# Value product split by head into single PSUM banks from batch 2 on, with two planner costs changed (causal attention followed by an MLP, one core)

## The chip, the cores and the metric

The kernel runs on one core of a Trainium2 chip. The metric is the device time in microseconds (us). TensorE (PE) does the matmuls, VectorE (DVE) and ScalarE (ACT) work on what they leave in PSUM, GpSimd (POOL) converts types and issues some loads, SyncE (SP) issues most of the DMA. PSUM, where matmuls write, is used as 8 banks of 512 float32 values in each of 128 partitions.

## The reference

Block-causal attention over 8 batches of 8 heads, 576 positions and a head size of 64, then an MLP with the activation h * sigmoid(beta * h) over all 4608 rows:

```
scores = q @ k^T / sqrt(64)                       # [8, 8, 576, 576]
scores = where(pos_i // 64 >= pos_j // 64, scores, -1e9)
attn   = softmax(scores)
x      = (attn @ v) as rows of 512 (8 heads x 64)  # [4608, 512]
h      = x @ w_in                                 # 512 -> 2048
g      = h * sigmoid(beta * h)
out    = g @ w_out                                # 2048 -> 512, float32
```

## The kernel before

**Two streams of work.** Attention runs over 32 units, one for each batch b and head pair c (u = 4b + c). The MLP runs over 9 chunks of 512 rows (r = 0 to 8). Attention's result is written transposed into xT, from which the chunks read; a chunk can start once the batches that hold its rows are done. Both streams are mixed on PE.

**One attention unit.** K and Q are converted to bfloat16 and transposed into QKT (in batches 0 and 1 by PE and a copy on DVE, from batch 2 on by DMA). The score product (L708, helper L443) works with 64-row tiles, the two heads of a pair side by side on the two halves of the array. It is done in visits: groups 0 to 2 of a unit take a pair of banks each, group 3 a small block in a single bank. From batch 2 on (JOIN) two units share three visits: groups 0 and 1 of the first, groups 2 and 3 of both, groups 0 and 1 of the second. ACT takes the exponential of a bank pair (L724, 128 x 1024) into E, DVE sets masked blocks to zero (L730, L732). The value product (L764) then multiplies E with V, full 128-row tiles, 15 matmuls of 65 columns for each head: 64 values and a row sum from a column of ones. Before the change both heads are one operation of 30 matmuls on a pair of banks. DVE takes reciprocals of the row sums (L776, 128 x 10) and multiplies (L783, 128 x 640) into xq; for unit 1 alone, ACT does the multiplication as ten scaled copies (L788). From batch 3 on a DMA transposes xq into xT (L800); in batches 0 to 2 PE transposes it (L813) and DVE, or ACT for units 2 and 3, copies it (L823, L821).

**One MLP chunk.** 16 groups of four matmuls of 512 columns (L1000), one bank each; ACT takes a tanh (L1010), DVE forms the gate gT (L1014), and the bank is free. The output product of chunk 0 is plain (L1036). Chunks 1 to 8 use a seven-product scheme on quadrants (function fast: products at L921, 8 matmuls of 256 columns for each half of rows; sums of quadrants on DVE at L885; results out of PSUM on ACT at L942 and DVE at L945 and L936). One of its banks is held through four products in a row, a second one for the others.

**What sets the order.** Class Plan holds a list scheduler that runs when the kernel is built. Each operation has engines, a duration, a latency, a priority and tiles; the scheduler goes forward in time and gives each free engine the ready operation of the lowest priority number. The order of each engine and the buffers' places are fixed by it; on the chip each engine goes through its own list and waits on semaphores. On PE a change between row tiles and full tiles costs the constant SWITCH (L53) in the plan, an operation of the other mode has 0.25 added to its priority number, and an operation counts as ready only SLACK (L54) after its inputs. Filler matmuls (L523, L525) are put in while PE has nothing else in the first 50 us.

**Banks.** The class of a PSUM tile decides where it may lie. "PP" is a pair, at the first free place of its list `at` (by default 0 or 2). "P1" is a single bank, and while any pair is still to come it may be one of 4 to 7 only (L246):

```
ok = [k for k in banks if k >= 4 or pairs == 0]
t.slot = next((k for k in ok if k ^ 1 not in banks), ok[0])
```

Score groups are PP at 0 or 2. The value product is PP with a list of its own (L754), from batch 2 on 0, 2, 4, 6 in this order. L1000, the output products, PE's transposes and the small score block are P1.

Of the kernel before, what the change touches and what calls it, by code (L numbers as in the profile page):

```python
# [4 lines left out]
ACT = mybir.ActivationFunctionType  # L5
# [43 lines left out]
class Plan:  # L49


    SEM = 70.0
    SWITCH = 140.0  # L53
    SLACK = 120.0  # L54
    LAND = 2600.0
    PKT, BOTH, LATE = 97.0, 0.87, 2000.0
# [303 lines left out]
def bass_blockwise_causal_attn__then__act_swish_beta_kernel(  # L360
# [10 lines left out]
    with es:  # L371
# [6 lines left out]
        PARTS = [((0, 4, "SP", range(6)), (4, 8, "SP", range(2)), (4, 8, "POOL", range(2, 6)))] + [((0, 8, "SP", range(6)),)] * 7  # L378
        GROUPS = [((0,), (1,), (2,), (3,))] + [((0, 1), (2, 3))] * 7
        NS = 6  # L380
        JOIN = (2,3,4,5,6,7)
        NO = 4
        FAST = range(1, NRC)
# [68 lines left out]
        def xq_(tx):  # L452
            return 3 if tx.cls == "XX" else tx.slot
# [147 lines left out]
        for u in range(NU):  # L601
# [157 lines left out]
            def fav(g, e, te=te, pv=pv, Tv=Tv, c=c):  # L759
                for h in range(2):  # L760
                    for i in range(5):
                        for t in range(i + 1):
                            o = PS[:, pv.slot + h, 65 * i:65 * i + 65]
                            z = g.matmul(o, eblk(te, t, i, h), Vn[Tv.slot][:, t, 2 * c + h, 0:65],  # L764
                                         start=(t == 0), stop=(t == i))
                return z
# [4 lines left out]
            def both(pv, n0, n1):  # L771
                a = PS[:, pv.slot, n0:n1]
                return bass.AP(a.tensor, a.offset, [a.ap[0], [512, 2], [65, 5], [1, n1 - n0]])

            def fr(g, e, pv=pv, ti=ti):
                return g.reciprocal(inv[ti.slot][:].rearrange("p (h i n) -> p h i n", h=2, n=1), both(pv, 64, 65))  # L776

            r = P.op("DVE", 150, fr, deps=[av], tiles=[pv, ti], prio=0)

            def fm(g, e, pv=pv, ti=ti, tx=tx):  # L780
                x = inv[ti.slot][:]
                x = bass.AP(x.tensor, x.offset, [x.ap[0], [5, 2], [1, 5], [0, 64]])
                return g.tensor_tensor(xq[xq_(tx)][:].rearrange("p i (h d) -> p h i d", h=2), both(pv, 0, 64), x,  # L783
                                       ALU.mult)
            def fa(g, e, pv=pv, ti=ti, tx=tx):
                for h in range(2):
                    for i in range(5):
                        z = g.activation(xq[xq_(tx)][:, i, 64 * h:64 * h + 64], PS[:, pv.slot + h, 65 * i:65 * i + 64],  # L788
                                         ACT.Copy, scale=inv[ti.slot][:, 5 * h + i:5 * h + i + 1])
                return z  # L790
# [339 lines left out]
```

## Time and profile before

| | |
|---|---|
| median of 4 runs | 333.69 us (333.17 to 336.76) |
| the profiled execution, its own time | 333.85 us |
| its span, first to last instruction | 332.0 us |
| granted TensorE clock | 1.00 |
| PE, DVE, ACT, POOL busy | 323.9, 220.9, 212.9, 85.2 us |
| L1000 | 576 matmuls of 512 columns |
| L921 | 896 matmuls of 256 columns |
| L764 (value product) | 960 matmuls of 65 columns |
| first L1000 starts at | 28.82 us |
| DMA engines' mean busy share | 0.9 or more from about 8 to 232 us, 0.2 or less after |

Lines of the profile name an engine, the line of the kernel, the operation, what is written and read, the shape and the count. Matmuls overlap, so the duration of one (379 ns for 512 columns) is longer than the distance from one start to the next; for the pace of PE the starts are what counts. A wait is put down to what came last before it ended. "issue" is time in which an engine waited for nothing that the profile shows.

### The profile page before, as it was taken

The page shows a single profiled execution, that of the slowest core. Times are in us where ns is not written, and L with a number is a line of the kernel's source. Part 1 is how long each engine was busy: PE and PEld are TensorE (multiplying, and loading weights), DVE is VectorE, ACT ScalarE, POOL GpSimd, SP SyncE. Part 2 cuts the span into 40 slices and gives each one's busy share as a digit, 9 for nine tenths or more (in the row PEclk, how much of TensorE's full clock was granted, in tenths as well). Part 3 has the DMA queues.
Part 4 walks back from the last instruction along what each step waited for, and adds up shares of the span by engine and source line. Part 5 has one row for each costly group of instructions (what it writes and reads, how often), then busy time and mean ns, then how long its engine had stood idle before and what let it go on. Part 6 is the DMA issues. An engine that isn't in the chain of part 4 may idle for free.

```text
span 332.0 us, 7512 instructions
## 1 busy us (share of the span) xinstructions
PE 323.9 (98%) x3146; PEld 203.8 (61%) x3090; DVE 220.9 (67%) x448; ACT 212.9 (64%) x324; POOL 85.2 (26%) x127
## 2 busy tenths in 40 slices
PE   7998999999999999999999999999999999999996
PEld 4574455545586457754765666576566766666685
DVE  4647875678653887358956694668467685666742
ACT  2876974297558886768657866874875555544521
POOL 7656082055074036103520631060000000000000
PEclk9999999999999999999999999999999999999999
DMA  7999999999999999999999999999102210110023
GB/s 210 226 233 235 187 210 210 202 280 211 185 258 203 205 231 195 194 214 200 174 173 221 240 207 185 171 179 167 35 34 40 86 51 34 53 43 32 1 96 126
DMA packets 154993, 53.41 MB, mean 161 GB/s; under 512 B 139072, under 2 KB 154448, under 8 KB 154960
## 3 DMA queue, kind: packets, MB, share of 16 engines
q1 hardware_dynamic: 141200, 40.19, 65.2%
q10 hardware_dynamic: 8192, 8.39, 8.5%
q0 software_dynamic: 5568, 4.36, 8.3%
q8 instruction: 24, 0.39, 0.5%
q14 instruction: 9, 0.07, 0.1%
HBM read 36.71 MB, written 9.44 MB: 139 GB/s over the span
## 4 chain that ended last, share of the span: by engine, by line
PE 91%; DMA 3%; ACT 2%; issue 1%; DVE 1%; SPq 1%; POOL 0%
PE PS L1000 38%; PE PS L921 29%; PE PS L708 8%; PE PS L764 8%; PE PS L1036 4%; DMA ST<-in_k_dram 2%; PE PS L525 1%; PE PS L813 1%; ACT E L724 1%; DMA xT<-xq 1%; PE PS L634 1%; ACT xq L788 1%; SPq L618 1%; ACT th L1010 0%; POOL QKn L625 0%
## 5 line engine op out<-in xcount | busy, mean ns | idle before, releaser
L1000 PE MATMUL PS<-xT,w_in 128*128 128x512 bf16 x576 | 136.6, 379 | 0.6 <-DMA xT<-xq 0.4
L1010 ACT ACTIVATE th<-PS,beta 128x512 f32<-128x512 f32 x144 | 96.6, 699 | 60.6 <-PE PS L1000 59.4
L1014 DVE SCALAR_TENSOR_TENSOR gT<-th,PS 128x512 f16<-128x512 f32 x144 | 95.1, 681 | 32.0 <-ACT th L1010 31.1
L724 ACT ACTIVATE E<-PS 128x1024 bf16<-128x1024 f32 x93 | 92.1, 1028 | 27.7 <-PE PS L708 27.7
L1000 PEld LDWEIGHTS PS<-xT,w_in 128*128 128x128 bf16 x576 | 53.3, 98 | 56.3 <-DVE gT L1014 2.0
L921 PE MATMUL PS<-w_out,gT 128*128 128x256 f16 x512 | 63.0, 273 | 0.0
L921 PEld LDWEIGHTS PS<-w_out,gT 128*128 128x128 f16 x512 | 49.0, 98 | 12.1 <-issue 1.3
L574 POOL CAST Vn<-Vs 128x640 bf16<-128x640 f32 (+1 forms) x28 | 22.3, 797 | 96.0 <-DMA Vs<-in_v_dram 94.6
L665 POOL CAST QKn<-ST 128x640 bf16<-128x640 f32 x48 | 36.4, 759 | 28.1 <-DMA ST<-in_k_dram 14.7
L708 PE MATMUL PS<-QKT 64*128 64x320 bf16 (+4 forms) x328 | 36.4, 297 | 0.2 <-ACT E L724 0.2
L764 PEld LDWEIGHTS PS<-Vn,E 128*128 128x128 bf16 x930 | 30.8, 97 | 3.9 <-DVE E L730 0.4
L942 ACT ACTIVATE ost<-PS 128x512 f32<-128x512 f32 x32 | 19.4, 606 | 21.5 <-PE PS L921 21.5
L921 PE MATMUL PS<-OV 128*128 128x256 f16 x256 | 31.9, 273 | 0.0
L764 PE MATMUL PS<-Vn,E 128*128 128x65 bf16 x930 | 31.9, 193 | 0.0
L708 PEld LDWEIGHTS PS<-QKT 64*128 64x128 bf16 (+1 forms) x328 | 13.4, 95 | 25.7 <-issue 11.2
L921 PEld LDWEIGHTS PS<-OV 128*128 128x128 f16 x256 | 24.2, 98 | 5.8 <-issue 1.1
L783 DVE TENSOR_TENSOR xq<-PS,inv 128x640 bf16<-128x640 f32 x30 | 24.6, 821 | 0.8
L885 DVE TENSOR_TENSOR OV<-gT 128x1024 f16<-128x1024 f16 x32 | 23.6, 744 | 1.1 <-PE PS L921 0.6
L730 DVE MEMSET E<- 64x64 uint32 x62 | 6.9, 112 | 23.8 <-ACT E L724 21.7
L945 DVE SCALAR_TENSOR_TENSOR ost<-PS,ost 128x512 f32<-128x512 f32 x22 | 15.1, 688 | 8.7 <-PE PS L921 6.2
L921 PE MATMUL PS<-OV,gT 128*128 128x256 f16 x128 | 16.1, 273 | 0.0
L1036 PE MATMUL PS<-w_out,gT 128*128 128x512 f16 x64 | 15.5, 380 | 0.0
(65 smaller groups left out, 175.3 us busy)
## 6 DMA issues: line engine op xcount, KB each, us to landing
out_dram<-ost ACTq DMA_DIRECT2D x32, 256.0 KB, 4.3
ST<-in_q_dram SPq DMA_DIRECT2D x12, 576.0 KB, 5.8
ST<-in_k_dram SPq DMA_DIRECT2D x12, 576.0 KB, 7.7
Vs<-in_v_dram SPq DMA_DIRECT2D x24, 256.0 KB, 5.0
ST<-in_q_dram SPq DMA_DIRECT2D x8, 288.0 KB, 6.4
ST<-in_k_dram SPq DMA_DIRECT2D x8, 288.0 KB, 6.8
w_in<-in_moe_w_in_dram POOLq DMA_DIRECT2D x4, 512.0 KB, 10.9
w_out<-in_moe_w_out_dram POOLq DMA_DIRECT2D x4, 512.0 KB, 9.7
```

Of the source, the lines that this page charges most:

```text
L574: return g.tensor_copy(Vn[t.slot][:, 0:n, g0:g1, 0:64], Vs[ts.slot][:, 0:n, g0:g1, :])
L665: return g.tensor_copy(QKn[tn.slot][:].rearrange("p a w n -> p (a w n)")[:, 640 * (2 * a + w):][:, 0:640] .rearrange("p (t h d) -> p t h d ...
L708: z = g.matmul(o, QKT[tqk.slot][r, uu % 2, 1, 128 * t + y:128 * t + m + y], x)
L724: return g.activation(E3[es_(te)][:, g0, :, :], PS[:, ps.slot:ps.slot + 2, :], ACT.Exp, scale=0.125)
L764: z = g.matmul(o, eblk(te, t, i, h), Vn[Tv.slot][:, t, 2 * c + h, 0:65], start=(t == 0), stop=(t == i))
L783: return g.tensor_tensor(xq[xq_(tx)][:].rearrange("p i (h d) -> p h i d", h=2), both(pv, 0, 64), x, ALU.mult)
L885: return P.op("DVE", dve_t(SZ * HC / 2), mk(lambda g: g.tensor_tensor(fo(), fx(), fy(), op)), deps=deps, tiles=tiles, prio=prio)
L921: x = g.matmul(PS[:, pw.slot, HM * w:HM * w + HM], fa()[:, j, 128 * w:128 * w + 128], fb()[:, j, :], start=first and (pair or w == 0) and ...
L1000: z = g.matmul(PS[:, ph.slot, :], w_in[:, c, 128 * j:128 * j + 128], xT[:, c, row % RX:row % RX + RC], start=(c == 0), stop=(c == 3))
L1010: return g.activation(th[tt.slot][:], PS[:, ph.slot, :], ACT.Tanh, scale=beta[:, j:j + 1])
L1014: return g.scalar_tensor_tensor(out=gT[tg.slot][:, j, :], in0=th[tt.slot][:], scalar=1.0, in1=PS[:, ph.slot, :], op0=ALU.add, op1=ALU.mult)
L1036: z = g.matmul(PS[:, po.slot, 0:d1 - d0], gT[tg.slot][:, j, 128 * w:128 * w + 128], w_out[:, j, d0:d1], start=(j == 0), stop=(j == NJ - 1))
```

## The change

From batch 2 on (HALVES) each head of the value product is an operation of its own: 15 matmuls into one P1 bank, then its own reciprocal of 5 row sums for each partition and its own multiplication of 320 values into the head's columns of xq. What follows (transposing xq) waits for both. In batches 0 and 1 the value product stays whole, on a PP tile. In the plan, a value matmul is set at 30 ns in place of 34, and SWITCH at 97 ns in place of 140. The scaled copies on ACT for unit 1 are gone; DVE does that multiplication as for the others.

```diff
-    SWITCH = 140.0
+    SWITCH = 97.0
...
+        HALVES = (2,3,4,5,6,7)
...
-            pv = P.tile("PP")
-            pv.at = (4, 6, 0, 2) if u in (2, 3) else (4, 6) if b < 1 else (0, 2, 4, 6) if b in JOIN else (0, 2)
+            whole = b not in HALVES
             ti, tx = P.tile("inv"), P.tile("XX" if u == 3 else "xq")
...
-            av = P.op("PE", 30 * 34, fav, deps=ex + zs + load[u], tiles=[te, Tv, pv, ti, tx],
-                      lat=30 * 34 + 180, mode="full", prio=pr(u)+.4 + 5 * (b < 1))
...
-            if u in (1,):
-                m = P.op("ACT", 1500, fa, deps=[av, r], tiles=[pv, ti, tx], lat=1700, prio=0)
-            else:
-                m = P.op("DVE", dve_t(640), fm, deps=[av, r], tiles=[pv, ti, tx], prio=0)
+            nrm = []
+            for hs_ in ((0, 1),) if whole else ((0,), (1,)):
+                pv = P.tile("PP" if whole else "P1")
+                pv.at = (4, 6, 0, 2) if u in (2, 3) else (4, 6) if b < 1 else (0, 2, 4, 6) if b in JOIN else (0, 2)
+
+                def fav(g, e, te=te, pv=pv, Tv=Tv, c=c, hs_=hs_):
+                    for h in hs_:
+                        for i in range(5):
+                            for t in range(i + 1):
+                                o = PS[:, pv.slot + h - hs_[0], 65 * i:65 * i + 65]
+                                z = g.matmul(o, eblk(te, t, i, h), Vn[Tv.slot][:, t, 2 * c + h, 0:65],
+                                             start=(t == 0), stop=(t == i))
+                    return z
+
+                nh = len(hs_)
+                av = P.op("PE", 15 * nh * 30, fav, deps=ex + zs + load[u], tiles=[te, Tv, pv, ti, tx],
+                          lat=15 * nh * 30 + 180, mode="full", prio=pr(u)+.4 + 5 * (b < 1))
...
+                def fr(g, e, pv=pv, ti=ti, hs_=hs_, both=both):
+                    x = inv[ti.slot][:, 5 * hs_[0]:5 * hs_[-1] + 5]
+                    return g.reciprocal(x.rearrange("p (h i n) -> p h i n", i=5, n=1), both(pv, 64, 65))
+
+                r = P.op("DVE", 150, fr, deps=[av], tiles=[pv, ti], prio=0)
+
+                def fm(g, e, pv=pv, ti=ti, tx=tx, hs_=hs_, nh=nh, both=both):
+                    x = inv[ti.slot][:, 5 * hs_[0]:5 * hs_[0] + 5]
+                    x = bass.AP(x.tensor, x.offset, [x.ap[0], [5, nh], [1, 5], [0, 64]])
+                    y = xq[xq_(tx)][:].rearrange("p i (h d) -> p h i d", h=2)[:, hs_[0]:hs_[-1] + 1]
+                    return g.tensor_tensor(y, both(pv, 0, 64), x, ALU.mult)
+                m = P.op("DVE", dve_t(320 * nh), fm, deps=[av, r], tiles=[pv, ti, tx], prio=0)
                 m.same = [r]
-            nrm = [m]
+                nrm.append(m)
```

More of the change, by code (lines that the diff above doesn't have):

```diff
@@ L757, in bass_blockwise_causal_attn__then__act_swish_beta_kernel @@
                 spare_x = tx
[L759 to L766, printed above, removed]
-            av = P.op("PE", 30 * 34, fav, deps=ex + zs + load[u], tiles=[te, Tv, pv, ti, tx],
-                      lat=30 * 34 + 180, mode="full", prio=pr(u)+.4 + 5 * (b < 1))
@@ L771, in both @@
[L771 to L790, printed above, removed]
-            if u in (1,):
-                m = P.op("ACT", 1500, fa, deps=[av, r], tiles=[pv, ti, tx], lat=1700, prio=0)
-            else:
-                m = P.op("DVE", dve_t(640), fm, deps=[av, r], tiles=[pv, ti, tx], prio=0)
+            nrm = []
@@ new lines, in bass_blockwise_causal_attn__then__act_swish_beta_kernel, with both @@
+            for hs_ in ((0, 1),) if whole else ((0,), (1,)):
[12 more added lines that the diff above has]
+                          lat=15 * nh * 30 + 180, mode="full", prio=pr(u)+.4 + 5 * (b < 1))
+                def both(pv, n0, n1, nh=nh):
+                    a = PS[:, pv.slot, n0:n1]
+                    return bass.AP(a.tensor, a.offset, [a.ap[0], [512, nh], [65, 5], [1, n1 - n0]])
+                def fr(g, e, pv=pv, ti=ti, hs_=hs_, both=both):
[8 more added lines that the diff above has]
+                m = P.op("DVE", dve_t(320 * nh), fm, deps=[av, r], tiles=[pv, ti, tx], prio=0)
```

## The prediction

> **What bounds the kernel now.** I read the page's table of engines first, then its slices, then the chain that ended last, and after that the waits of TensorE alone.
>
> ```profile
> PE 323.9 (98%) x3146; PEld 203.8 (61%) x3090; DVE 220.9 (67%) x448; ACT 212.9 (64%) x324; POOL 85.2 (26%) x127
> ...
> PE   7998999999999999999999999999999999999996
> ...
> PE 91%; DMA 3%; ACT 2%; issue 1%; DVE 1%; SPq 1%; POOL 0%
> ```
>
> TensorE (PE) is busy in nearly every slice but the first four and the last, and it carries 91% of the chain. No other engine is above 67%. A busy PE need not be a full PE, so the second view is where PE waited at all:
>
> ```profile
> PE PS L523 <- POOL identF L459: 2.4, 1, 2.4
> PE PS L813 <- issue: 1.1, 1, 1.1
> ...
> PE PS L1000 <- DMA xT<-xq: 0.4, 1, 0.4
> ```
>
> Those few microseconds are nearly all there is. The third view is the order of time on PE, to see whether the matmuls follow each other at their own rate:
>
> ```profile
> 107.27 1.07 PE L764 MATMUL PS<-Vn,E 128*128 128x65 bf16 x30
> 108.17 2.75 PE L1000 MATMUL PS<-xT,w_in 128*128 128x512 bf16 x12
> 110.86 0.39 PE L708 MATMUL PS<-QKT 64*128 64x512 bf16 x2
> 111.08 0.19 PE L443 MATMUL PS<-QKT 64*128 64x64 bf16 x2
> 111.11 0.35 PE L708 MATMUL PS<-QKT 64*128 64x448 bf16 x2
> 111.40 0.82 PE L1000 MATMUL PS<-xT,w_in 128*128 128x512 bf16 x3
> ```
>
> Start to start, the value product's 30 matmuls take 108.17 - 107.27 = 0.90 us, 30 ns each. The chain has eight matmuls of L1000 in 1.73 us, 216 ns each; so the 12 here should take 2.59 us, and the score product (L708) starts 2.69 us after their start: 0.10 us for the change of tile mode. The way back costs the same: 111.40 - 111.11 is 0.29 us, of which two 448-column matmuls side by side account for about 0.19 us. Doing this sum for every neighbouring pair from 30 us on leaves only five gaps of 0.15 us or more: 0.55 us at 202.5 (input of chunk 5 not landed), 0.43 at 53.0, 0.25 at 99.7, 0.17 at 44.3 and 0.15 at 34.8, together 1.55 us. So after 30 us the time is the number of matmuls, plus mode changes, plus 1.55 us. Before 30 us PE waits for data, exponentials and normalised rows; the first L1000 starts at 28.82 us.
>
> **What the Trainium skill says.** TensorEngine Tiling (Array Packing), Key Properties: changing the tiling mode drains TensorE. The trace agrees, with 0.10 us each way. PSUM — Partial Sum Buffer, the section on bank collisions: two engines may not use one bank at once. So VectorE (DVE) can only read a finished head while PE works on the other because each has its own bank; no collision is in this trace. Perfetto Trace Analysis, Optimizing Scalar/DVE Operations: if the vector engine isn't saturated but causes bubbles on other engines, smaller instructions may complete work sooner. Here the first half holds (67%), but the trace has hardly any bubble on PE to remove.
>
> **The change part by part.** I sum against the profiled execution's own 333.85 us (span 332.0 and 1.85 around it); the median of the runs shown is 333.69, 0.16 less.
>
> *Numbers of the planner.* Mode change 140 to 97 ns and 34 to 30 ns for a value matmul cost no time on the chip; they are what the trace above shows. They move the order on PE. Every visit of the score product in batches 2 to 7 needs both bank pairs 0-1 and 2-3, and each can be filled again only after two exponentials of 1.03 us (L724), so visits cannot join: three for each two head pairs, 36 in all, 72 mode changes or about 7 us, before and after. The gain open here is the gaps from orders planned with wrong times: at most 1.55 us. I take 0.9 of it, the gap at 202.5 and a part of the rest, since that one is a landing that was due by a slow plan of PE. Ends: 0 and 1.55.
>
> *Two half products.* The same 30 matmuls, 0.45 us for each half. In this trace the matmuls of one operation follow those of another at the normal rate, so 24 more borders cost PE nothing in themselves. What is new is the place: a half asks for one of banks 4 to 7, which L1000, the output products and the small score block share, where the pair mostly lay in 0 to 3.
>
> *Normalising on DVE.* From the groups kept apart by form:
>
> ```profile
> L783 DVE TENSOR_TENSOR xq<-PS,inv 128x640 bf16<-128x640 f32 x30 | 24.6, 821 | 0.8
> L945 DVE SCALAR_TENSOR_TENSOR ost<-PS,ost 128x512 f32<-128x512 f32 x22 | 15.1, 688 | 8.7 <-PE PS L921 6.2 <-ACT ost L942 2.3
> L776 DVE RECIPROCAL inv<-PS 128x10 f32<-128x10 f32 x32 | 6.9, 216 | 10.3 <-PE PS L764 10.0
> L936 DVE SCALAR_TENSOR_TENSOR ost<-PS,ost 128x256 f32<-128x256 f32 x4 | 1.6, 423 | 5.9 <-ACT ost L942 4.0 <-PE PS L921 2.0
> ```
>
> No row has 320 elements from PSUM. Between 256 and 512 elements the time grows by (688 - 423) / 256 = 1.035 ns each, so 320 should take 423 + 64 x 1.035 = 489 ns; the same line gives 820 for 640, against the 821 measured. A reciprocal of 5 I leave at about 0.21 us. A unit then costs 2 x (0.49 + 0.21) = 1.40 us of DVE, where it cost 0.82 + 0.22 = 1.04. Times 24 units this is +8.6 us, and with head pair 1 of batch 0 (below) DVE comes to 230 us, 69%. PE's matmuls hide it: in the stretch from 60 to 262 us DVE is busy 140 of 202 us. If the cover were gone, the whole 8.6 us would show. In exchange a unit's rows are finished about 0.3 us sooner, since the last half needs 0.70 us after PE where the whole needed 1.04; nothing on PE waits for that.
>
> *The wait that is added.* The second half waits for a bank of its own. PE's order is fixed, so everything behind it waits too, and then ScalarE (ACT), whose tanh lives from L1000. I bound it from bank time. An L1000 group holds its bank from 108.17 to the end of its gate at about 110.64, 2.5 us, for 0.87 us of PE. A half should hold its bank 0.45 + 0.2 (PE's end to the reciprocal) + 0.21 + 0.05 + 0.49 = 1.4 us, and 2.1 us if one gate multiplication (L1014, 0.68) stands ahead of it on DVE. The four banks serve PE without a stop as long as a group holds less than four times its PE time: 2.5 against 3.5 for L1000, 1.4 to 2.1 against 1.8 for halves. Only where output products keep two of the four does it get narrow. I take 0.3 us over the whole kernel; ends 0 and 5 (worked out under the rival). A gain is excluded here: banks 0 to 3 coming free earlier can only fill gaps on PE, and those are counted above.
>
> *Head pair 1 of batch 0.* Its ten scaled copies leave ACT for one multiplication on DVE. The chain at the start:
>
> ```profile
> 23.21 2.17 ACT xq L788 x10
> 25.38 0.14 issue
> 25.52 0.52 PE PS L813 x5
> 26.03 0.36 PE PS L634 x6
> 26.39 0.11 PE PS L813 x2
> 26.50 1.10 issue
> 27.61 0.42 PE PS L813 x3
> ...
> 28.05 0.72 ACT xT L821 x2
> ```
>
> ACT's 2.17 us are on this chain only because the transposes of pair 1 stand ahead of those of pair 3. DVE's own row of events ends pair 3's multiplication at 25.20 + 0.82 = 26.02 us, so without ACT the chain could start again at about 26.1 and not at 25.5: nothing is won that way. DVE in turn does about 5 us of work between 21.7 and 27.3 us and gets 0.82 us more, which pushes pair 3's by 0.3 to 1.1 us (a copy to xT can slip in front of it). The 1.10 us marked "issue" then cover a part, if PE waits there for its own instructions and not for data. I take +0.3 us; ends -1.1 (the issue gap goes) and +1.1.
>
> *Sum:* 333.85 - 0.9 + 0.3 + 0.3 = 333.55, say 333.5 us.
>
> **The rivals.** *Later start* (0.14): the whole 1.1 us on DVE reach the first L1000 and no gap goes: 333.85 + 1.1 = 334.95 us. For it speaks how full DVE is from 21.7 to 27.3; against it the 1.10 us issue gap behind which it may hide.
>
> *Banks 4 to 7 run short* (0.20), the case on the other side. Where output products hold two banks, a unit's halves hold the other two, and no L1000 can start until the first is free. In that time PE surely has the two halves and one output step (8 matmuls of L921, 0.87 us): 0.45 + 0.45 + 0.87 = 1.77 us. Once a half holds its bank longer than that, PE stands. At 2.1 us it is 0.33 us for each unit, and if 14 of the 24 meet such a moment, 14 x 0.33 = 4.6 us: 338.5 us. For it: between 60 and 262 us the next L1000 comes whenever a bank is free, so the banks are well used, and DVE gets more queue. Against: the planner knows the banks and has score products to put there, and 0-3 come free of value products.
>
> *A better start and no gaps* (0.10): the issue gap of 1.1 us goes, the chain through pair 3 loses another 1.0 us because the shorter planned products bring its product forward, and all of the 1.55 us goes: 333.85 - 3.65 = 330.2 us. For it: all three are seen in the profile. Against: three things at once, and DVE's queue.
>
> That the order hardly changes, so that the planner's new numbers do nothing, is part of the likeliest case and would give about 334.
>
> **How the numbers follow.** The likeliest case, PE without gaps as before, has 0.56 and its own range of 332.0 to 335.5. About 1%, 3.3 us, is what a measurement of this kernel can tell from no change. Faster by over that needs below 330.4: most of the last case, 0.07. Slower by over it needs above 337.0: the bank case and a tail of the start, 0.21. The rest is 0.72. The range takes in half of the fast case and all but the upper third of the bank case: 330.9 to 338.0.
>
> **What would show each step right or wrong.** Right: PE's waits after 30 us still below 2 us in all; mode changes unchanged at about 0.10 us; the value product in groups of 15 matmuls of 30 ns; twice as many reciprocals for the units of batches 2 to 7 and multiplications of 320 elements at about 0.49 us; DVE near 230 us; the gap at 202.5 smaller. The start: first L1000 between 27.7 and 29.9 us. Wrong: waits of L1000 or L764 for DVE of some tenths each, many of them, between 60 and 262 us would mean the bank case. The whole is wrong if the span without the start grows or shrinks by more than 2 us with PE still gapless, since then the work itself or its number of mode changes isn't what I counted.

## The result and the profile after

The kernel after takes 336.48 us (median of 42 runs, 335.09 to 340.63), the kernel before, measured beside it, 334.68 us (63 runs). The ratio is 1.0059 with a 95% interval of 1.0042 to 1.0076: the change costs about 2 us. That is inside the 1% that the prediction called "no change" and inside its range of 330.9 to 338.0. But the prediction's sum, 333.55 from 333.85, was a small gain, and the measured change is a loss. The profiled execution took 337.57 us (span 335.8); a single profiled execution of any of these kernels can lie some us from its median, since the granted clock is 0.99 in some and transfers land earlier or later, so the ratios decide and the profiles only tell where.

In the kernel after, the value product is L768, its multiplication L790, its reciprocal L782, the score product L709, the exponential L725, L1000 is L996, L921 is L917, the gate L1014 is L1010, and the sums of quadrants L885 are L881. The page's engine table, the slices of PE and the chain that ended last:

```profile
PE 326.5 (97%) x3153; PEld 207.2 (62%) x3097; DVE 225.9 (67%) x497; ACT 212.7 (63%) x314; POOL 85.2 (25%) x127
...
PE   7998999999999999999999999999999999999996
...
PE 84%; DVE 4%; ACT 3%; SPq 2%; DMA 2%; issue 1%; POOL 1%; POOLq 0%; ACTq 0%
```

PE is as full as before in tenths, yet its share of the chain fell from 91% to 84%, and DVE and ACT have 4% and 3% where they had 1% and 2%. The time went to many small places. The waits of PE alone (total us, times, longest):

```profile
PE PS L996 <- DVE xq L790: 1.2, 3, 0.6
PE PS L709 <- ACT E L725: 0.7, 1, 0.7
PE PS L635 <- POOL QKn L626: 0.7, 1, 0.7
...
PE PS L1032 <- DVE xT L819: 0.3, 1, 0.3
```

The first line is new: L996, the MLP's first product, waits for a half's multiplication, that is for the bank that the half still holds. The wait for the DMA into xT (0.4 us before, at 202.5) is gone, as predicted.

The groups by form have the two new shapes:

```profile
L790 DVE TENSOR_TENSOR xq<-PS,inv 128x320 bf16<-128x320 f32 x48 | 22.9, 485 | 0.9
L782 DVE RECIPROCAL inv<-PS 128x5 f32<-128x5 f32 x48 | 8.8, 187 | 4.4 <-PE PS L768 3.8
```

485 ns were worked out as 489, and 187 ns taken as 210. And one of the new waits in the order of time:

```profile
135.84 1.07 PE L768 MATMUL PS<-Vn,E 128*128 128x65 bf16 x30
...
136.45 0.96 DVE L881 TENSOR_TENSOR gT<-gT,OV 128x1024 f16<-128x1024 f16 x1
...
137.34 0.18 DVE L782 RECIPROCAL inv<-PS 128x5 f32<-128x5 f32 x1
137.38 1.05 PE L917 MATMUL PS<-OV 128*128 128x256 f16 x8
137.44 1.10 DVE L881 TENSOR_TENSOR gT<-gT,OV 128x1024 f16<-128x1024 f16 x1
...
138.46 0.48 DVE L790 TENSOR_TENSOR xq<-PS,inv 128x320 bf16<-128x320 f32 x1
...
139.00 1.25 PE L996 MATMUL PS<-xT,w_in 128*128 128x512 bf16 x5 [0.57 <-DVE xq L790]
```

(The 30 value matmuls are the two halves of one pair, one behind the other.) PE is through with them at about 136.8, but the first half's multiplication starts at 138.46 only, because two quadrant sums of 0.96 and 1.10 us stand ahead of it in DVE's order. This half's bank is held from 135.84 to 138.94, 3.1 us, and L996 stands behind it. Over all 48 halves the hold (first matmul to the end of the multiplication) is 1.37 to 3.69 us, 2.04 in the middle, and over 2.1 us in 20 of them.

To compare whole kernels I use one number worked out from each trace: the time lost on PE between 40 and 300 us. From each operation's first matmul to that of the next is its time; off it go its matmuls at the pace that undisturbed neighbours show (216 ns for 512 columns, 109 for 256, 29.3 for the value product, and so on) and 0.096 us for a change of mode. The rest is lost. The sum has an offset common to all kernels (score visits run a little longer than so reckoned), so only differences count: before 6.77 us, after 9.16, a difference of +2.4, about the whole loss. Before 40 us the profiled execution of after lost another 1.6 us, but its V arrived 1.4 us later than in the one of before (conversion at 21.12 instead of 19.72). That varies between executions: with after's order kept (e6_thin below) the conversion was at 20.51, with before's order kept (e13_dve_halves below) at 20.82.

### The profile page after: what moved, and what is told of

Read it like the earlier page. It is cut to its first block, busy times and chain, and to the rows that moved or that the text cites. A ratio compares the mean times of both kernels' runs of the same rounds, so it can differ in the third digit from the quotient of the medians.

```text
span 335.8 us, 7554 instructions
## 1 busy us (share of the span) xinstructions
PE 326.5 (97%) x3153; PEld 207.2 (62%) x3097; DVE 225.9 (67%) x497; ACT 212.7 (63%) x314; POOL 85.2 (25%) x127
## 4 chain that ended last, share of the span: by engine, by line
PE 84%; DVE 4%; ACT 3%; SPq 2%; DMA 2%; issue 1%; POOL 1%; POOLq 0%; ACTq 0%
PE PS L996 35%; PE PS L917 28%; PE PS L768 8%; PE PS L709 7%; PE PS L1032 4%; DMA Vs<-in_v_dram 2%; SPq L549 2%; ACT E L725 2%; ACT th L1006 1%; PE PS L809 1%; DVE gT L1010 1%; DVE gT L881 1%; DVE OV L881 1%; PE PS L635 1%; DVE xq L790 1%
## 5 line engine op out<-in xcount | busy, mean ns | idle before, releaser
L996 PE MATMUL PS<-xT,w_in 128*128 128x512 bf16 x576 | 137.2, 379 | 1.3 <-DVE xq L790 1.2
L1010 DVE SCALAR_TENSOR_TENSOR gT<-th,PS 128x512 f16<-128x512 f32 x144 | 95.8, 681 | 40.1 <-ACT th L1006 39.2
L725 ACT ACTIVATE E<-PS 128x1024 bf16<-128x1024 f32 x93 | 92.2, 1027 | 24.7 <-PE PS L709 24.7
L996 PEld LDWEIGHTS PS<-xT,w_in 128*128 128x128 bf16 x576 | 53.6, 98 | 55.8 <-DVE xq L790 2.1
L917 PE MATMUL PS<-w_out,gT 128*128 128x256 f16 x512 | 63.4, 273 | 0.0
L917 PEld LDWEIGHTS PS<-w_out,gT 128*128 128x128 f16 x512 | 49.0, 98 | 11.9 <-issue 1.3
L666 POOL CAST QKn<-ST 128x640 bf16<-128x640 f32 x48 | 37.9, 789 | 40.3 <-DMA ST<-in_k_dram 22.8
L575 POOL CAST Vn<-Vs 128x640 bf16<-128x640 f32 (+1 forms) x28 | 20.9, 748 | 85.5 <-DMA Vs<-in_v_dram 84.1
L709 PE MATMUL PS<-QKT 64*64 64x64 bf16 (+4 forms) x328 | 36.5, 297 | 0.7 <-ACT E L725 0.7
L768 PEld LDWEIGHTS PS<-Vn,E 128*128 128x128 bf16 x930 | 31.8, 97 | 5.5 <-issue 0.8
L768 PE MATMUL PS<-Vn,E 128*128 128x65 bf16 x930 | 33.9, 193 | 0.4 <-POOL Vn L575 0.4
L917 PE MATMUL PS<-OV 128*128 128x256 f16 x256 | 32.2, 273 | 0.0
L790 DVE TENSOR_TENSOR xq<-PS,inv 128x320 bf16<-128x320 f32 (+1 forms) x55 | 28.6, 528 | 1.1
L917 PEld LDWEIGHTS PS<-OV 128*128 128x128 f16 x256 | 24.4, 98 | 6.8 <-issue 0.8
L709 PEld LDWEIGHTS PS<-QKT 64*128 64x128 bf16 (+1 forms) x328 | 13.4, 95 | 24.2 <-issue 11.4
L881 DVE TENSOR_TENSOR OV<-gT 128x1024 f16<-128x1024 f16 x32 | 23.1, 726 | 0.4
L733 DVE MEMSET E<- 64x128 uint32 x31 | 5.1, 165 | 17.3 <-ACT E L725 16.3
L917 PE MATMUL PS<-OV,gT 128*128 128x256 f16 x128 | 16.1, 273 | 0.0
```

The lines of the kernel that those rows point to most:

```text
L575: return g.tensor_copy(Vn[t.slot][:, 0:n, g0:g1, 0:64], Vs[ts.slot][:, 0:n, g0:g1, :])
L666: return g.tensor_copy(QKn[tn.slot][:].rearrange("p a w n -> p (a w n)")[:, 640 * (2 * a + w):][:, 0:640] .rearrange("p (t h d) -> p t h d ...
L709: z = g.matmul(o, QKT[tqk.slot][r, uu % 2, 1, 128 * t + y:128 * t + m + y], x)
L725: return g.activation(E3[es_(te)][:, g0, :, :], PS[:, ps.slot:ps.slot + 2, :], ACT.Exp, scale=0.125)
L790: return g.tensor_tensor(y, both(pv, 0, 64), x, ALU.mult)
L881: return P.op("DVE", dve_t(SZ * HC / 2), mk(lambda g: g.tensor_tensor(fo(), fx(), fy(), op)), deps=deps, tiles=tiles, prio=prio)
```

## Experiments: one part of the change at a time

My first theory was that each part has its own cost: the numbers of the planner a gain, the halves a wait on banks 4 to 7, head pair 1 a later start. The rival was that one of them alone makes the loss.

**PE's two numbers alone** (e1_numbers; before, nothing else changed).

```diff
-    SWITCH = 140.0
+    SWITCH = 97.0
...
-            av = P.op("PE", 30 * 34, fav, deps=ex + zs + load[u], tiles=[te, Tv, pv, ti, tx],
-                      lat=30 * 34 + 180, mode="full", prio=pr(u)+.4 + 5 * (b < 1))
+            av = P.op("PE", 30 * 30, fav, deps=ex + zs + load[u], tiles=[te, Tv, pv, ti, tx],
+                      lat=30 * 30 + 180, mode="full", prio=pr(u)+.4 + 5 * (b < 1))
```

> The kernel before with the planner's two numbers alone (mode change 97 ns, value matmul 30 ns); value product whole, ten scaled copies still on ACT. Bank theory (halves in banks 4 to 7 make PE wait for DVE to give banks back): no change, ratio 0.998 to 1.002. Numbers theory (the old, too high costs gave the other engines a margin in the plan, and the exact ones take it away): slower by 1.5 to 2.3 us, 1.0045 to 1.007, with new gaps on PE after 30 us. Start theory (head pair 1 on DVE delays the first L1000): no change.

Measured: ratio 1.0178 [1.0135, 1.0221], almost 6 us slower and outside what any of the three theories gave. The numbers are nearer to the trace than the old ones, and the loss is three times that of after. Waits of PE:

```profile
PE PS L1000 <- DMA xT<-xq: 1.6, 1, 1.6
...
PE PS L708 <- ACT E L724: 1.1, 1, 1.1
PE PS L708 <- DVE xq L783: 0.9, 3, 0.3
PE PS L1000 <- DVE E L730: 0.8, 1, 0.8
```

Before had 0.4 us in the first of these. The new order starts chunk 4 of the MLP before its rows have landed (1.6 us at 181), and its score visits meet banks that a whole value product still holds. So the planner's numbers are no gain of 0.9 us by themselves.

**Halves and pair 1 without the numbers** (e2_halves; after, with the old ones).

```diff
-    SWITCH = 97.0
+    SWITCH = 140.0
...
-                av = P.op("PE", 15 * nh * 30, fav, deps=ex + zs + load[u], tiles=[te, Tv, pv, ti, tx],
-                          lat=15 * nh * 30 + 180, mode="full", prio=pr(u)+.4 + 5 * (b < 1))
+                av = P.op("PE", 15 * nh * 34, fav, deps=ex + zs + load[u], tiles=[te, Tv, pv, ti, tx],
+                          lat=15 * nh * 34 + 180, mode="full", prio=pr(u)+.4 + 5 * (b < 1))
```

> The changed kernel with the old numbers of the planner (140 and 34 ns). Bank theory: the whole loss stays, 1.5 to 2.3 us, 1.0045 to 1.007, with waits of PE for DVE's multiplication of a half. Numbers theory: no change to before, 0.998 to 1.002. Start theory: a part, 0.5 to 1.2 us (1.0015 to 1.0035).

Measured: 1.0169 [1.0131, 1.0207]. Waits of PE:

```profile
PE PS L768 <- DMA xT<-xq: 1.7, 1, 1.7
PE PS L996 <- ACT E L737: 1.2, 1, 1.2
PE PS L709 <- DMA QKT<-QKn: 0.8, 1, 0.8
...
PE PS L996 <- DVE xq L790: 0.3, 1, 0.3
```

Nearly the same loss as the numbers alone, again outside all that was expected, and the wait for a half is one of the smallest in the view. Two parts that cost 6 us each and 2 us together are no parts of a sum. That was the end of the first theory's bookkeeping.

**Head pair 1 on DVE alone** (e3_pair1; before).

```diff
-            if u in (1,):
+            if u in ():
                 m = P.op("ACT", 1500, fa, deps=[av, r], tiles=[pv, ti, tx], lat=1700, prio=0)
```

> The kernel before with head pair 1 of batch 0 normalised on DVE and nothing else changed. Start theory: slower by 0.5 to 2 us (1.0015 to 1.006), the first L1000 later than 28.8 us by as much. Bank and numbers theory: no change, 0.999 to 1.001.

Measured: 1.0053 [1.0032, 1.0073], 1.8 us slower. Lost on PE from 40 us on: +0.4 only; up to 40 us +1.1. Before's wait for a landing, 0.4 us at 202.5, is gone, and a longer one stands at 175 us:

```profile
PE PS L1000 <- DMA xT<-xq: 0.9, 1, 0.9
```

An edit of the first 30 us has moved a wait for a landing far behind it.

**Pair 1 given back to ACT** (e5_act; after).

```diff
-                m = P.op("DVE", dve_t(320 * nh), fm, deps=[av, r], tiles=[pv, ti, tx], prio=0)
+                if u in (1,):
+                    m = P.op("ACT", 1500, fa, deps=[av, r], tiles=[pv, ti, tx], lat=1700, prio=0)
+                else:
+                    m = P.op("DVE", dve_t(320 * nh), fm, deps=[av, r], tiles=[pv, ti, tx], prio=0)
```

> The changed kernel with the ten scaled copies of head pair 1 given back to ACT. Start theory (DVE's queue before the first L1000 costs 1 to 1.9 us in the changed kernel too): ratio to before falls to 1.001 to 1.004. Bank theory (the loss is PE waiting for banks that halves hold): the start costs nothing in this plan, so the ratio stays at 1.006 to 1.008, with waits of L1000 for a half's multiplication as in the changed kernel. Order theory (each new plan meets new waits of any kind): anywhere from 1.000 to 1.015, with gaps at other places.

Measured: 1.0077 [1.0044, 1.0109], no better than after, as the bank theory had it; the order theory's range takes it in too. What cost 1.8 us when it was put into before wins nothing when it is taken out of after. From about the 435th matmul on, PE's list of instructions is after's own here, so this kernel is less a new order than after's behind another start.

**Halves in any bank** (e4_low; after; a half may lie in banks 0 to 3 too, lowest first).

```diff
-                    ok = [k for k in banks if k >= 4 or pairs == 0]
+                    ok = [k for k in banks if k >= 4 or pairs == 0 or any(t.low for t in o.tiles if t.slot is None)]
...
-                                ok = [k for k in banks if k >= 4 or pairs == 0]
-                                t.slot = next((k for k in ok if k ^ 1 not in banks), ok[0])
+                                ok = sorted(banks) if t.low else [k for k in banks if k >= 4 or pairs == 0]
+                                t.slot = ok[0] if t.low else next((k for k in ok if k ^ 1 not in banks), ok[0])
...
+                pv.low = not whole
```

> The changed kernel, but a half product may lie in any of the eight banks, the lowest free one first, so that it takes banks 0 to 3 as the whole product did. Bank theory: most of the loss goes, ratio to before 0.999 to 1.002, and PE's gaps after 30 us come down from about 3.9 us to 2 or less. Numbers theory: the loss stays, 1.0045 to 1.007. Start theory: 1.0015 to 1.0035 stays.

Measured: 1.0079 [1.0043, 1.0115]. In the program, 41 of the 48 halves lie in banks 0 to 3, where after has 2. The view of PE's waits lists none for a half's multiplication any more (1.2 us in after), and its longest one behind the start is

```profile
PE PS L998 <- DVE E L732: 0.8, 1, 0.8
```

PE lost 1.2 us more than before in the middle instead of 2.4, yet the kernel is not faster than after. So the wait for banks 4 to 7 can be removed without getting the time back. But this edit changes the plan too: PE's list leaves after's behind the 774th matmul, so what the banks alone are worth is not told apart from the other order.

## Experiments: DVE later than its plan

The second theory: banks are held too long since DVE runs later than the planner thinks. A quadrant sum is planned at 0.66 us and takes 0.73 to 0.75 on average, 0.96 and 1.10 in the timeline above.

**Thin quadrant sums with the plan kept**, in after (e6_thin) and, as its control, in before (e7_thin_before). 32 of the 64 sums do a quarter of their columns; the rest of these sums is left out. (w is HC, all columns, unless given.)

```diff
-                    fo(), fx(), fy(), op)), deps=deps, tiles=tiles, prio=prio)
+                    fo()[:, :, 0:w], fx()[:, :, 0:w], fy()[:, :, 0:w], op)), deps=deps, tiles=tiles, prio=prio)
...
-                         gs[SZ * i:SZ * i + SZ] + gs[HJ + SZ * i:HJ + SZ * i + SZ] + [SS[3][i]], [tg])
+                         gs[SZ * i:SZ * i + SZ] + gs[HJ + SZ * i:HJ + SZ * i + SZ] + [SS[3][i]], [tg], w=HC // 4)
...
-                         [SS[2][i]] + p2 + hi, [tg, t2])
+                         [SS[2][i]] + p2 + hi, [tg, t2], w=HC // 4)
```

> The changed kernel with its plan kept, order and banks alike, but the quadrant sums that write into gT (32 of 64 instructions) do only a quarter of their columns, so the output products there are not those of the reference; DVE is relieved of some 15 us. Bank theory with DVE as the cause: the halves' multiplications come sooner, PE's waits for banks held by halves (1.7 us in the changed kernel) fall to 0.5 or less, ratio to before 1.001 to 1.004. If those waits have another cause: they stay, ratio 1.006 to 1.008.

> The control: the kernel before with its plan kept and the same 32 sums on a quarter of their columns (again not the reference's products). Bank theory: PE of the kernel before waits for DVE for less than 0.5 us after 30 us, so next to nothing is won, ratio 0.998 to 1.000. If a lighter DVE helps any plan alike: ratio lower by as much as between the changed kernel and its thinned form, 0.995 to 0.997.

Measured: after's order 1.0042 [1.0015, 1.0069], before's order 0.9990 [0.9961, 1.0020]. In after's order the two rows of thinned sums went from 751 and 754 ns to 286 and 387. The wait at 139 went; 1.7 of the 2.4 us lost in the middle stayed. Before's order gained 0.5 us there from the same thinning, after's 0.7. The ratio of after's order, 1.0042, lies just outside the 1.001 to 1.004 that the bank theory gave, and its interval takes in after's own 1.0059. So a DVE that is less late is worth little in either, and hardly more in after's.

**The planner told of DVE's times** (e8_dve; after).

```diff
-                r = P.op("DVE", 150, fr, deps=[av], tiles=[pv, ti], prio=0)
+                r = P.op("DVE", 200, fr, deps=[av], tiles=[pv, ti], prio=0)
...
-                return P.op("DVE", dve_t(SZ * HC / 2), mk(lambda g: g.tensor_tensor(
+                return P.op("DVE", 750, mk(lambda g: g.tensor_tensor(
```

> The changed kernel with two more of the planner's numbers set by the profile: 200 ns for a reciprocal in place of 150, 750 ns for a quadrant sum in place of 663. Theory that the bank waits come from DVE being planned too fast: waits of PE for a half's multiplication fall from 1.7 to 0.6 us or less, ratio to before 1.001 to 1.004. Order theory: the plan changes everywhere, other waits come up, ratio anywhere from 1.000 to 1.015.

Measured: 1.0023 [1.0000, 1.0045], and only +0.2 us lost in the middle. It looked like the cure. But the halves hold their banks as long as in after: 1.98 us in the middle against 2.04, over 1.77 in 32 of 48 against 33. Also the wait for them is still there:

```profile
PE PS L996 <- DVE xq L790: 0.8, 2, 0.6
```

So the same numbers were tried in three other places: in before (e9_before_dve); in after without halves, where HALVES is empty (e10_whole_dve); and in e8_dve with pair 1 back on ACT as in e5_act (e11_dve_act). A fourth kernel, e12_dve900, is e8_dve with the sum at 900 in place of 750. The first edit below is what e10_whole_dve has beside the two numbers, the second is e12_dve900's against e8_dve.

```diff
-        HALVES = (2,3,4,5,6,7)
+        HALVES = ()
...
-                return P.op("DVE", 750, mk(lambda g: g.tensor_tensor(
+                return P.op("DVE", 900, mk(lambda g: g.tensor_tensor(
```

> The kernel before with two planner numbers of DVE corrected and nothing else: a reciprocal 200 ns in place of 150, a quadrant sum 750 in place of about 660. If a DVE that is later than its plan was the loss, before had little of it (two waits of its own, 0.44 and 0.25 us), so this should be 0 to 1 us faster than before. If the order that comes out of any changed number costs by itself, it should be 1 to 5 us slower, as it was when the two numbers of PE alone were changed (+4.7).

> The kernel after with the DVE numbers of e8_dve and no halves: HALVES empty, so every value product stays whole on a pair of banks; PE's two numbers and pair 1 on DVE as in after. If the halves themselves are worth something once the plan knows DVE, this is slower than e8_dve (+1.0 us on before) by 1 us or more. If the halves are only a cost of DVE and of banks, it is as fast or faster, 0 to 1 us on before. With PE's numbers alone and DVE's wrong the whole product stood at +4.7.

> e8_dve with head pair 1 of batch 0 given back to ACT's ten scaled copies. If pair 1 on DVE costs the start 1 to 2 us here as it did in before's plan, this is 1 to 2 us faster than e8_dve, so 0 to 1 us faster than before. If it costs nothing in this plan, as in after's, it stays at +1.0 within 0.5.

> e8_dve with the quadrant sum set higher still, 900 ns in place of 750: sums beside a POOL cast took 0.96 and 1.10 us. If what counts is that the plan is not too early on DVE, this is no slower than e8_dve: +0 to +1 us on before, and PE waits for a half's multiplication under 0.3 us. If 750 was a lucky order, it goes back to after's +2.5 us.

(The +4.7 and +1.0 us that these expectations take for PE's numbers alone and for e8_dve are what the medians of executions at full clock show; the ratios above, over all executions, give 5.9 and 0.8.)

Measured, in this order: 1.0053 [1.0025, 1.0081], 1.0044 [1.0020, 1.0067], 1.0091 [1.0057, 1.0126] and 1.0200 [1.0137, 1.0263]. The same correction makes before slower by 1.8 us, and the step from 750 to 900 ns, in the direction that should help, costs about 6 us. A part of this is the clock: e12_dve900 ran four times, never with a granted clock of 1.00, and against executions of before at the same 0.995 three of its four give 1.0150, which leaves about 4 us for the step. Waits of PE in the last one:

```profile
PE PS L996 <- DMA xT<-xq: 2.3, 1, 2.3
PE PS L635 <- issue: 1.6, 1, 1.6
PE PS L709 <- DMA QKT<-QKn: 1.0, 1, 1.0
...
PE PS L996 <- DVE xq L790: 0.4, 1, 0.4
```

PE waits for transfers now. The second theory falls as a cause; that 750 did well looks like luck of the order and not like a better plan of DVE. With whole products and the same numbers (e10_whole_dve) the loss is 1.5 us against e8_dve's 0.8, and their intervals overlap: no gain or loss of the halves can be told. Pair 1 back on ACT (e11_dve_act) is 3 us slower than before, which neither branch of its expectation had.

## Experiments: the order itself

The third theory: what costs is the new order, whatever made it new. A list scheduler decides each next operation by times that lie close together, so a number changed anywhere gives another order from there on; before's order happens to meet few waits. The rival: the halves, their DVE work or nearness of the numbers to the trace have a cost of their own. This can be told apart by changing the work with the order kept, and the order with the work kept.

**Work changed, order kept** (e13_dve_halves; before, with every engine's order, the banks and the planner's numbers as they were; DVE takes the two heads of a unit one after the other from batch 2 on).

```diff
+            HV = ((0, 1), (1, 2)) if b >= 2 else ((0, 2),)  # DVE takes the heads one by one
...
-                return g.reciprocal(inv[ti.slot][:].rearrange("p (h i n) -> p h i n", h=2, n=1), both(pv, 64, 65))
+                return [g.reciprocal(inv[ti.slot][:, 5 * h:5 * k].rearrange("p (h i n) -> p h i n", i=5, n=1), both(pv, 64, 65)[:, h:k]) for h, k in HV][-1]
...
-                return g.tensor_tensor(xq[xq_(tx)][:].rearrange("p i (h d) -> p h i d", h=2), both(pv, 0, 64), x,
-                                       ALU.mult)
+                y = xq[xq_(tx)][:].rearrange("p i (h d) -> p h i d", h=2)
+                return [g.tensor_tensor(y[:, h:k], both(pv, 0, 64)[:, h:k], x[:, h:k], ALU.mult) for h, k in HV][-1]
```

> The kernel before with its whole plan kept (order of every engine, banks, PE's numbers), but from batch 2 on DVE takes a unit's two heads one after the other: two reciprocals of 5 and two multiplications of 320 in place of one and one. That is DVE's part of the change alone: 24 x (2 x 0.187 + 2 x 0.485 - 0.216 - 0.821) = +7.4 us of DVE, with no new bank and no new order. If DVE's extra work is what costs, this is 1 us or more slower than before. If PE's matmuls hide it and only the order counts, it is within 0.3 us.

Measured: 1.0004 [0.9976, 1.0032]. The groups by form:

```profile
L784 DVE TENSOR_TENSOR xq<-PS,inv 128x320 bf16<-128x320 f32 x48 | 21.2, 484 | 0.6
L776 DVE RECIPROCAL inv<-PS 128x5 f32<-128x5 f32 x48 | 6.2, 170 | 6.0 <-PE PS L764 5.8
```

48 of each, as in after, and the time is before's; lost in the middle 6.75 us against 6.77. DVE's part of the change costs nothing in before's order, as far as the interval of about 1 us either way can tell. (This kernel keeps the whole product's bank pair, so the choice of banks isn't in it.)

**Order changed, work kept.** Before with SWITCH 130 (e14_sw130) and with 150 (e15_sw150), where it had 140; after with 96 (e16_sw96) and with 99 (e17_sw99), where it had 97; and before with 139 (e18_sw139), which moves one short stretch on PE (a value product, four L1000, an output product and two transposes around the end of chunk 0) and leaves PE's order behind it as it was. The edit of the first, of which the others are copies:

```diff
-    SWITCH = 140.0
+    SWITCH = 130.0
```

> The kernel before with SWITCH 130 in place of 140 and nothing else. The number is no better founded than 140, but the list of PE comes out different in most of its length. If any new order costs because before's is a good draw, this is 1 to 5 us slower. If orders are about equal and after lost by what its numbers say, it is within 1 us of before.

> The kernel before with SWITCH 150, further from the 97 that the trace shows. Good draw: 1 to 5 us slower, as for 130. If numbers nearer to the trace are what makes the orders worse (a plan with a PE too slow leaves room), 150 is within 1 us of before or faster, and 130 is slower.

> The kernel after with SWITCH 96 in place of 97, nothing else: 1 ns, which no trace can tell apart, but PE's list comes out different in most of its length. If after's +2.5 us belong to the halves, this is +2 to +3 us on before again. If they belong to the draw of the order, it can be anywhere between 0 and +5, and differs from after by 1 us or more.

> The kernel after with SWITCH 99 in place of 97: a third draw of the changed kernel, whose list on PE differs from after's in about the length of a third. If the orders are draws around one mean, +1 to +4 us on before. If after's halves are a loss of fixed size, +2 to +3.

> The kernel before with SWITCH 139 in place of 140: on PE only one short stretch around the output products of chunk 0 and the first of chunk 1 comes in another order (a value product, four L1000 and an output product change places), everything behind it is as before. If what counts is how much of before's order is kept, this is within 1 us of before. If any edit of a number costs, 1.5 to 3 us slower.

Measured:

| kernel | PE's order | ratio to before | lost in the middle, minus before's |
|---|---|---|---|
| before, SWITCH 130 | new | 1.0055 [1.0027, 1.0083] | +1.8 us |
| before, SWITCH 150 | new from the middle on, little before | 1.0078 [1.0051, 1.0105] | +0.8 |
| after (97) | new | 1.0059 [1.0042, 1.0076] | +2.4 |
| after, 96 | new | 1.0051 [1.0028, 1.0073] | +2.7 |
| after, 99 | new, in its first half after's | 1.0059 [1.0036, 1.0082] | +2.1 |
| before, SWITCH 139 | kept but for one stretch | 1.0003 [0.9973, 1.0034] | -0.5 |
| before, heads apart on DVE | kept | 1.0004 [0.9976, 1.0032] | 0.0 |
| before, thin sums | kept | 0.9990 [0.9961, 1.0020] | -0.5 |

Ten nanoseconds on one planner number, in either direction, with the same work, cost as much as the whole change. One expectation came out in neither way: after with 96 was to lose 2 to 3 us if the halves cost, or to differ from after by 1 us or more if the order did. By its ratio it lost 1.7 us and differs from after by 0.3. And these three are not free draws: with 99 PE's list is after's up to the 1639th of 3153 matmuls.

Executions also differ in their granted clock (last section), and those of before had it reduced more often than some others. Among executions at full clock alone the ratios are 1.0061 (130), 1.0101 (150), 1.0085 (96), 1.0092 (99), 1.0001 (139), 1.0007 (heads apart) and 1.0000 (thin sums). New and kept orders lie further apart in this count, not closer. After with 96 and with 99 then lose 2.9 and 3.1 us, about what their expectations gave for halves that cost; before with 130 and 150, which has no halves, loses 2.0 and 3.4.

The loss sits elsewhere in each. Waits of PE with 130:

```profile
PE PS L1000 <- ACT ost L942: 0.9, 1, 0.9
PE PS L1000 <- DVE E L732: 0.8, 1, 0.8
```

and in after with 96:

```profile
PE PS L709 <- ACT E L725: 0.7, 1, 0.7
...
PE PS L996 <- DVE gT L1010: 0.4, 1, 0.4
PE PS L768 <- DVE xq L790: 0.4, 1, 0.4
```

Of the first, nothing is in the change's reach: results of the output product and masked blocks of E. The rival about nearness to the trace fails too, since 150, farther from 97 than 140, is no better than 130.

With after, fifteen kernels of this study have a new order on PE. In thirteen of them at most 4 in 10 matmuls lie in stretches of 60 or more that before has too, in e3_pair1 and with SWITCH 150 nearly 6 in 10. They are not fifteen independent orders, since some share long stretches with after or with e8_dve. All fifteen are slower than before, by 0.2% (e8_dve, whose interval just touches 1) to 2.0% (1.5% for the last with the clocks matched); the middle one of them is after itself, 1.0059. Six have whole products (numbers alone, pair 1 alone, DVE's numbers in before and in after without halves, 130, 150): 1.0044 to 1.0178. Nine have halves: 1.0023 to 1.0200. The two sets lie over each other; their middles, 1.0054 and 1.0077, are 0.8 us apart, too little to tell with so few. The three kernels that keep before's order, or all of it but a stretch, are all within 0.1% of it, each to about 0.3%. No kernel here is faster than before beyond its interval.

## Why the prediction was wrong

**The bound and the matmuls: right.** PE is full, has 3153 instructions where it had 3146, and goes between score products and other matmuls 112 times where it did 110 times. The gap at 202.5 went. The halves are groups of 15 at the same pace.

**DVE: right in the parts, too high in the sum.** 485 and 187 ns against 489 and 210. DVE came to 225.9 us, not 230: neighbouring instructions overlap, and with two heads back to back the order-keeping kernel shows 222.2 us in all, 1.3 more than before. That PE's matmuls hide it is shown, in before's order, by its 1.0004. The Trainium skill's advice in Perfetto Trace Analysis, Optimizing Scalar/DVE Operations, that smaller instructions can finish work sooner, is not put to the test here: there was no bubble of that kind to remove.

**Numbers of the planner, -0.9 us (ends 0 and -1.55): this step failed.** It counted the gaps that the old order has and took a part of them away, as if a new plan could only lose gaps. A new plan is a new list, which brings its own. The numbers alone brought +5.9 us (about 5 at full clock), numbers of no better footing (130, 150) +1.8 and +2.6. If the other two terms are left at +0.3 each, the measured loss of 2.0 us leaves +1.4 for this one; that is a remainder and not a measurement, since the parts do not add up. A term that fits these runs would be about +2 with ends of 0 and +6, which is known only now. The same flaw is in the sentence that the order hardly changes: PE's list in after leaves before's at the 60th matmul, and 96 in place of 97 changed it again from the 159th on.

**The added wait, +0.3 us (ends 0 and 5): too small for this order.** 1.2 us of L996 waiting for halves in the view of waits. The hold was bounded at 2.1 us by one gate ahead on DVE; two quadrant sums of a microsecond each can stand there too, and 20 of 48 holds are over 2.1. But the hold doesn't decide as the rival "Banks 4 to 7 run short" had it. That rival had the direction and a kind of wait that is really in the trace; its point of 1.77 us is passed in 32 of 48 cases by e8_dve, which loses 0.2 us in the middle. So a long hold does not cost by itself; that it costs only where the order asks for the bank just then fits the traces, but no run isolates it. Removing those waits (halves in any bank) gave nothing back, in a plan whose order changed with it.

**The start, +0.3 us (ends -1.1 and +1.1): not settled.** Before 40 us after lost 1.6 us more than before, of which 1.4 may be its later V. Pair 1 on DVE alone cost 1.8 us, given back it won nothing; it can't be told from the new order that comes with it. The first L1000 at 31.40 us is later than the 29.9 given. But before's own 28.82 us, on which that figure rests, was an early one: four other kernels with before's order on PE up to that point started it at 29.13 (e9_before_dve), 30.90, 30.96 and 30.97 us (thin sums, heads apart, 139). So the prediction took the start of one execution for the start of the kernel.

**What stays open.** That a new order alone can cost what this change cost is shown. That after's own 2 us come from its order and not from its halves is argued from that: no run has the halves on banks 4 to 7 with the order kept. After with 96, 97 and 99 gave nearly one loss, 1.0051 to 1.0059, which a fixed cost of the halves would do as well as a shared order, so such a cost of 1 us or so is not excluded. That before's order is better than the others is measured; why is not. An order that was kept because it measured well, out of many, would look like this, but no run here shows how it came about. Whether halves would win with an order found in that way wasn't tried; the nearest, with DVE's numbers at 200 and 750, is at 1.0023 [1.0000, 1.0045].

## What to carry to other kernels

In a kernel whose order comes out of a list scheduler, an edit of any number, or of any operation's length, can be first of all a new draw of the order. Compare the lists before and after: 139 in place of 140 moved one stretch and cost nothing, 130 moved most and cost 1.8 us. Where the list is new, give it a cost of its own with both ends, taken from plans with a number changed that means nothing, before the edit's own effect. To learn what an edit is worth, change the work with the order kept, and the order with the work kept. A wait that the profile names is where this order loses; removing it is no promise that the next order doesn't lose as much elsewhere.

## What the runs showed of the hardware that was not expected

The "issue" gap of PE at the start, which the prediction hoped might hide DVE's work, sits at one place in the count and not in the work. Sixteen of the twenty kernels here have it right after the 705th recorded instruction of PE (350 weight loads, 349 matmuls and 6 others in before), whatever stands there: a transpose of xq in before, one of Q or K in after. It begins between 25.7 and 27.9 us and lasts 0.4 to 2.6 us from start to start; with the same order on PE up to there it was 1.3 us in before and 1.4, 1.4, 2.3 and 2.6 in four others. The other four kernels do not have it. From the chain of waits of e13_dve_halves, and of after:

```profile
27.49 2.04 issue
```

```profile
28.13 0.48 issue
```

The Trainium skill, Runtime: NRT & Kernel Launch, Instruction fetch mechanics, says that an engine's instructions are fetched in blocks of 256 and that crossing a block is mostly hidden. A fetch would fit a gap that depends on the number of instructions and not on data. But no gap of that kind lies 256 instructions behind it, so that it is a fetch is not shown. With one order on PE it differs by 1.3 us between executions, so the starts of two single executions can't be compared.

A second thing at the start is the granted clock. Of the twenty profiled executions eight have a stretch at half the clock that begins between 28.7 and 31.1 us, just where the MLP starts: 3.41 us long in six, 6.83 us in two. It shows as an 8 in the fourth slice of e7_thin_before, where before has none:

```profile
PEclk9999999999999999999999999999999999999999
```

```profile
PEclk9998999999999999999999999999999999999999
```

In that execution the stretch goes from 29.6 to 33.0 us at a clock of 0.50, and the mean over the whole is 0.995. If PE is full then, half of 3.41 us is lost, an estimate of 1.7 us; the executions of before at 0.995 took 335.5 to 335.9 us on average in the five measurements beside the experiments, those at full clock 333.5 to 334.3. Only e12_dve900 has a second such stretch, at 180 us. So times of kernels compare best at the same clock, and the time lost between 40 and 300 us is free of it in all kernels but that one. What starts the stretch in one execution and not in another is not shown.
